# Other priorities for a list-scheduled kernel: attention and two MLPs on one core

## The chip, the cores and the metric

One core of a Trainium2 chip. The metric is the device time of one execution in microseconds (us). The kernel before took 796.75 us, the median of three runs (796.06 to 797.55).

## What is computed

The reference has three parts, one behind the other, all in fp32:

- block-causal attention: 4 batches, 8 heads, 576 positions, 64 channels per head, masked in blocks of 64 positions, softmax over the row;
- an MLP over the 2304 tokens: 512 to 1024 channels, `h * softmax(h)`, a layer norm with the gain `g_ln`, 1024 to 512 channels;
- a second MLP: 512 to 2048 channels, `h * cos(h)`, 2048 to 512 channels.

```python
x = attn(q, k, v)                 # 2304 x 512
h = x @ w_in                      # 2304 x 1024
solu = h * softmax(h)
ln = (solu - mean) / sqrt(var + 1e-6) * g_ln
y = ln @ w_out                    # 2304 x 512
h2 = y @ w2_in                    # 2304 x 2048
out = (h2 * cos(h2)) @ w2_out     # 2304 x 512
```

The weights reach the device as 64-bit words. The kernel turns each piece of 128 x 512 into fp32 and splits it into a high and a low part, and it multiplies activations and weights, both split so, in three products per matmul (high x high, high x low, low x high).

## The kernel before

**A list scheduler writes the order.** Every piece of work is registered with `op(...)` (`Scheduler.op`): the engines that may do it with a planned cost on each, what it reads and writes, and a priority. `Scheduler.run` then plays a planned clock forward. Whenever an engine of the plan is free, `pick` takes from that engine's list the first operation that is ready and whose tiles find a buffer; the list is sorted by the priority less `off(o, e)`, so a lower number goes first. Each engine's instructions are emitted in that order, SP's DMA queue (`q`) included. The order is fixed when the program is built; on the chip an engine never overtakes in its own queue.

The numbers that the plan uses stand in the dictionary `P`:

- `tile`, one number for each of the 18 token tiles of 128, is added to the tile's due time (`tile_pr`). It sets when the first layer (`trace_l1`, line 678), the transposes of the normalised tile (`trace_lnT`, line 711) and, four tiles together, the second layer (`trace_l2`, line 732, with `l2` and `l2_step`) come up.
- `lead0` to `lead7` and `pair` are taken off the due time of one pair of heads in one of eight attention groups; `prep` moves its loads (`trace_prep`) ahead.
- `att_pe`, `att_vec`, `att_slope`, `mlp_pe`, `mlp_vec` shift attention against the first MLP, on TensorE and on the other engines (`off`).
- `w_in`, `w_out`, `w_out_step`, `w2_direct`, `w2_step` are the due times of the weight conversions (`trace_weight`, lines 635 to 649).
- `weight` multiplies the planned costs where an operation may go to one of several engines (`p` TensorE, `s` ACT, `v` VectorE, `g` GpSimd): an engine leaves an operation to another that would end it earlier by these weighted costs. The evictions of the transposes (lines 327 and 331) are such operations.
- `stick` is how far down its list TensorE may look for an operation of the kind that it has just done.

```python
def off(self, o, e):
    kinds = {t.cls for t in o.tiles}
    if kinds & {"rw", "t1", "rwx", "t1x"}:
        return 0.0
    if kinds & {"e1", "LN", "yb", "psh", "st"}:
        return P["mlp_pe"] if e == "p" else P["mlp_vec"]
    if kinds & {"e", "eT", "us", "rq", "rk", "rv", "xs"}:
        return (P["att_pe"] if e == "p" else P["att_vec"]) - P["att_slope"] * o.prio
```

**The stages.** Attention runs in eight groups of four pairs of heads. Groups 0 to 3 are the late 320 rows of the four batches, groups 4 to 7 the early 256 rows (the short groups; their due times start at 200.8, 243.8, 275.8 and 307.8 thousand). A pair loads q, k and v (line 321), scales q (line 333), multiplies q and k (lines 495, 498, 530), takes row maxima (506), exponentials (509), scales them (522 or 524), transposes (581, evicted by 327 or 331) and multiplies with v (606). The result goes into a ring of five tiles XS, `xs_t[n]` in place `n % 5`, from which the first layer reads; tile n of the first layer and tile n + 5 of attention share a place. First-MLP work starts as soon as its tiles are there, and fills TensorE between attention steps. Its results go to DRAM (yD) and come back as chunks of up to 512 tokens.

The second MLP runs in two halves of eight pieces of 128 hidden channels, over five chunks: hidden layer (`trace_h2`, 771), cosine (`trace_cos`: ACT 782, VectorE 783, 785, 787, 789, ACT 791, VectorE 792, then the split at 331 and 336), output (`trace_out`, 811). Its due times start at 373.8 thousand, and each piece of the hidden layer waits for its weights and for the output of four pieces earlier. Its buffers, and most of those of its weights, are opened when the last attention operation has been placed.

The plan knows that VectorE and GpSimd block each other: an operation with `port=True` on VectorE does not start in the plan while a GpSimd one runs, and the reverse.

Where the plan sees TensorE idle before 70 us, small stand-in matmuls (line 953) are emitted.

Of the kernel before, what the change touches and what calls it, by code (L numbers as in the profile page):

```python
# [28 lines left out]


P = {
    "stick": 24783.0,
    "tile": [-14359.3, -37985.7, 6113.4, -3055.7, 24465.2, 4623.7, 3526.9, -32896.1, -22525.7, 27230.1, -18199.6, 22478.0, 37632.5, 59648.4, -15097.6, 596.8, -22562.3, -32058.0],
    "pair": [-10908.6, 3875.9, 1648.0, 792.0],
    "weight": {"p": 1.0, "s": 2.385, "v": 2.75, "g": 1.376, "q": 1.0},
    "att_slope": 0.053,
    "att_pe": 74866.7,
    "att_vec": 151894.2,
    "mlp_pe": -14159.9,
    "mlp_vec": 34158.7,  # L40
    "w_in": -10429.3,
    "w_out": 307495.7,
    "w_out_step": 1138.4,
    "w2_direct": 73027.9,
    "w2_step": 12920.1,
    "lead0": 7512.5,
    "lead1": 22625.7,
    "lead2": 8969.7,
    "lead3": -7974.6,
    "lead4": -9446.8,  # L50
    "lead5": -67400.4,
    "lead6": -7144.6,
    "lead7": -13408.6,
    "l2": 5241.5,
    "l2_step": 15170.5,
    "prep": 36287.5,
}


# [927 lines left out]
```

## Time and profile before

| | |
|---|---|
| time, median of three runs | 796.75 us |
| the profiled execution's own time | 796.97 us |
| its span, first to last instruction | 795.2 us |
| TensorE (PE) busy | 784.4 us, 99% |
| VectorE (DVE) busy | 588.0 us, 74% |
| ACT busy | 421.8 us, 53% |
| GpSimd (POOL) busy | 219.2 us, 28% |
| data moved by DMA | 86.79 MB, mean 109 GB/s |

Busy times are of the profiled execution; matmuls are pipelined, and their ends are modelled. Times within the trace count from the span's start. PEclk is the TensorE clock that was granted, as a share of 2.4 GHz.

### The profile page before, as it was taken

What the parts mean: (1) busy time and instruction counts of PE and PEld (TensorE: products, weight loads), DVE (VectorE), ACT (ScalarE), POOL (GpSimd) and SP (SyncE); (2) the same over time, 40 slices, a digit from 0 to 9 for tenths busy, and PEclk for the clock granted to TensorE, in tenths of its full rate; (3) what the DMA queues carried; (4) which work ended last, traced back from release to release, by engine and by line L of the source; (5) the groups of instructions that cost most, each with busy time, mean ns of one, the idle gap of its engine ahead of it and who ended that gap; (6) DMA issues with size and microseconds to landing.
All of it is one profiled execution on the core that took longest, in us unless ns stands there. A gap on an engine that the chain in (4) does not pass through costs nothing.

```text
span 795.2 us, 12231 instructions
## 1 busy us (share of the span) xinstructions
PE 784.4 (99%) x4291; PEld 622.1 (78%) x4291; DVE 588.0 (74%) x1238; ACT 421.8 (53%) x944; POOL 219.2 (28%) x320
## 2 busy tenths in 40 slices
PE   8999999999999999999999999999999999999998
PEld 5566666767888777889887778889988888888996
DVE  6989998664643774689879999667766676767775
ACT  6987997655433784476354555343434333333332
POOL 2675544412111553555634542000000000000000
PEclk9999999999999999999999999999999999999999
DMA  8435433322112221624385423022415032131121
GB/s 284 155 96 193 138 109 127 109 79 68 41 53 99 81 68 40 234 104 146 115 300 207 133 85 127 11 100 75 149 51 196 3 109 78 54 132 43 51 79 41
DMA packets 46030, 86.79 MB, mean 109 GB/s; under 512 B 4240, under 2 KB 18576, under 8 KB 45968
## 3 DMA queue, kind: packets, MB, share of 16 engines
q1 hardware_dynamic: 45968, 86.00, 32.5%
q8 instruction: 34, 0.56, 0.3%
q14 instruction: 28, 0.23, 0.1%
HBM read 67.11 MB, written 18.87 MB: 108 GB/s over the span
## 4 chain that ended last, share of the span: by engine, by line
PE 86%; DVE 4%; DMA 3%; ACT 2%; POOL 2%; issue 1%; SPq 0%; ACTq 0%; POOLq 0%
PE banks L771 22%; PE banks L811 22%; PE banks L732 13%; PE banks L678 11%; PE banks L606 6%; PE banks L581 5%; PE banks L495 4%; DMA rq<-qT 3%; PE banks L530 2%; PE banks L711 2%; POOL e L524 1%; DVE tr L787 1%; DVE gt L336 1%; DMA rw<-w_out 1%; POOL t L641 0%
## 5 line engine op out<-in xcount | busy, mean ns | idle before, releaser
L678 PE MATMUL banks<-w,XS 128*128 128x512 f32 x432 | 110.5, 401 | 0.0
L331 ACT ACTIVATE gt<-ta 128x512 fp32r<-128x512 f32 (+1 forms) x80 | 47.0, 588 | 110.0 <-PE banks L811 72.0
L732 PE MATMUL banks<-LN,w 128*128 128x512 f32 (+1 forms) x480 | 103.8, 372 | 0.0
L732 PEld LDWEIGHTS banks<-LN,w 128*128 128x128 f32 x480 | 83.1, 189 | 15.1 <-DVE LN L336 0.2
L678 PEld LDWEIGHTS banks<-w,XS 128*128 128x128 f32 x432 | 78.0, 188 | 18.6 <-issue 3.4
L811 PE MATMUL banks<-w,gt 128*128 128x512 f32 x378 | 91.8, 390 | 0.0
L641 POOL TENSOR_TENSOR t<-t,rw 128x512 uint32<-128x512 uint32 x45 | 63.8, 1419 | 80.3 <-DVE t L639 21.4
L782 ACT ACTIVATE ta<-banks 128x512 f32<-128x512 f32 (+1 forms) x80 | 44.3, 554 | 77.5 <-PE banks L771 76.0
L811 PEld LDWEIGHTS banks<-w,gt 128*128 128x128 f32 x378 | 70.8, 188 | 14.1
L783 DVE TENSOR_SCALAR ta<-ta 128x512 f32<-128x512 f32 (+1 forms) x80 | 37.1, 463 | 59.3 <-ACT ta L782 59.1
L509 ACT ACTIVATE e<-banks,us 128x384 f32<-128x384 f32 (+3 forms) x128 | 66.3, 530 | 20.0 <-DVE us L506 18.0
L791 ACT ACTIVATE ta<-tr,hpi 128x512 f32<-128x512 f32 (+1 forms) x80 | 53.9, 673 | 37.5 <-DVE tr L789 37.4
L506 DVE TENSOR_REDUCE us<-banks 128x1 f32<-128x384 f32 (+3 forms) x128 | 56.0, 481 | 14.8 <-PE banks L498 11.0
L336 DVE TENSOR_TENSOR gt<-ta,gt 128x512 fp32r<-128x512 f32 (+1 forms) x80 | 54.0, 675 | 16.4 <-ACT gt L331 15.6
L811 PE MATMUL banks<-wa,gt 128*128 128x512 f32 x270 | 65.7, 390 | 0.0
L792 DVE TENSOR_TENSOR ta<-banks,ta 128x512 f32<-128x512 f32 (+1 forms) x80 | 50.8, 636 | 12.3 <-ACT ta L791 11.9
L581 PE MATMUL banks<-ident,e 128*128 128x128 f32 x400 | 58.7, 278 | 1.1 <-POOL e L524 0.7
L524 POOL TENSOR_SCALAR e<-e,us 128x384 f32<-128x384 f32 (+3 forms) x97 | 49.1, 518 | 37.8 <-ACT e L509 20.4
L331 ACT ACTIVATE eT<-banks 128x512 f32<-128x512 f32 (+3 forms) x104 | 50.4, 525 | 16.0 <-PE banks L581 15.3
L811 PEld LDWEIGHTS banks<-wa,gt 128*128 128x128 f32 x270 | 50.5, 188 | 10.1
L581 PEld LDWEIGHTS banks<-ident,e 128*128 128x128 f32 x400 | 45.4, 140 | 16.0 <-POOL e L524 4.5
L787 DVE SCALAR_TENSOR_TENSOR tr<-ta,tr 128x512 f32<-128x512 f32 (+1 forms) x80 | 55.3, 692 | 2.2
(127 smaller groups left out, 1428.9 us busy)
## 6 DMA issues: line engine op xcount, KB each, us to landing
rw<-w_out SPq DMA_DIRECT2D x24, 512.0 KB, 3.6
rw<-w_in SPq DMA_DIRECT2D x22, 512.0 KB, 3.9
yD<-YB SPq DMA_DIRECT2D x16, 512.0 KB, 2.9
wa<-yD SPq DMA_DIRECT2D x7, 1024.0 KB, 7.6
rk<-kT SPq DMA_DIRECT2D x16, 288.0 KB, 3.7
oD<-ob SPq DMA_DIRECT2D x18, 256.0 KB, 2.4
ob<-oD SPq DMA_DIRECT2D x18, 256.0 KB, 3.3
rv<-vm SPq DMA_DIRECT2D x16, 256.0 KB, 2.9
```

The source lines that it names most:

```text
L331: S.activation(dst, src, AF.Copy, scale=1.0 if scale is None else scale)
L336: (V if eng == "v" else G).tensor_tensor(out=dst, in0=src, in1=h.bitcast(F32), op=ALU.subtract)
L506: op({"v": c_v(W)}, lambda _, h=h: V.tensor_reduce(out=us.ap[:, h:h + 1], in_=scs[h](), axis=AX.X, op=ALU.max, negate=True), [keys[h]], [( ...
L509: op({"s": c_s(W, True, True)}, lambda _, h=h: S.activation(e.ap[:, h, :], scs[h](), AF.Exp, bias=us.ap[:, h:h + 1], scale=1.0, accum_out= ...
L524: G.tensor_scalar(out=a, in0=a, scalar1=us.ap[:, 6 + h:7 + h], scalar2=1.0, op0=ALU.mult, op1=ALU.mult)
L581: PE.transpose(ps.ap[:, 128 * k:128 * k + 128], s(), ident)
L641: op({"g": c_g2(512)}, lambda _: G.tensor_tensor(out=t1.ap, in0=t1.ap, in1=lw(), op=ALU.add), [(rw, 0)], [t1], prio)
L678: PE.matmul(h.ap[:, 512 * c:512 * c + 512], lhsT=xs.ap[:, a, kt, :], rhs=w[:, b, 512 * c:512 * c + 512], start=(kt == 0 and a == 0 and b = ...
L732: PE.matmul(y.ap, lhsT=w[:, a], rhs=LN[:, b, kf, s0_:s0_ + len(t), :], start=(kf == 0 and a == 0 and b == 0), stop=(kf == 7 and b == 1))
L771: PE.matmul(ps.ap, lhsT=w[:, a, 128 * kt:128 * kt + 128], rhs=yts[q, c][kt // 2].ap[:, kt % 2, b, :], start=(k == 0), stop=(k == 11))
L787: op({"v": c_v(n)}, lambda _: V.scalar_tensor_tensor(out=r.ap, in0=a.ap, scalar=-TWO_PI_B, in1=r.ap, op0=ALU.mult, op1=ALU.add), [a], [r], ...
L811: PE.matmul(acc[x][1](), lhsT=gt.ap[:, a, 128 * x:128 * x + 128], rhs=w[:, b, 512:1024], start=(f % 8 == 0 and k == 0), stop=(f % 8 == 7 a ...
```

## The change

Only numbers of `P` differ. No operation, shape, buffer or planned cost is touched; `off`, `pick` and the rest are the same.

```diff
 P = {
-    "stick": 24783.0,
-    "tile": [-14359.3, -37985.7, 6113.4, -3055.7, 24465.2, 4623.7, 3526.9, -32896.1, -22525.7, 27230.1, -18199.6, 22478.0, 37632.5, 59648.4, -15097.6, 596.8, -22562.3, -32058.0],
-    "pair": [-10908.6, 3875.9, 1648.0, 792.0],
-    "weight": {"p": 1.0, "s": 2.385, "v": 2.75, "g": 1.376, "q": 1.0},
-    "att_slope": 0.053,
-    "att_pe": 74866.7,
-    "att_vec": 151894.2,
-    "mlp_pe": -14159.9,
-    "mlp_vec": 34158.7,
-    "w_in": -10429.3,
-    "w_out": 307495.7,
-    "w_out_step": 1138.4,
-    "w2_direct": 73027.9,
-    "w2_step": 12920.1,
-    "lead0": 7512.5,
-    "lead1": 22625.7,
-    "lead2": 8969.7,
-    "lead3": -7974.6,
-    "lead4": -9446.8,
-    "lead5": -67400.4,
-    "lead6": -7144.6,
-    "lead7": -13408.6,
-    "l2": 5241.5,
-    "l2_step": 15170.5,
-    "prep": 36287.5,
+    "stick": 25785.0,
+    "tile": [-37328.3, -83398.7, -19632.4, -6490.1, 22733.9, 11990.0, 16388.8, -15445.7, 4165.2, 47041.7, 14800.1, 26813.9, 32499.4, 56385.3, -32530.7, -2698.7, 16954.9, -23382.4],
+    "pair": [1070.3, 6128.5, 5113.2, 5181.4],
+    "weight": {"p": 1.0, "s": 2.696, "v": 2.758, "g": 1.374, "q": 1.0},
+    "att_slope": 0.1,
+    "att_pe": 78195.4,
+    "att_vec": 59571.4,
+    "mlp_pe": -27189.1,
+    "mlp_vec": -35603.7,
+    "w_in": -7521.5,
+    "w_out": 464087.8,
+    "w_out_step": 22213.3,
+    "w2_direct": 259837.4,
+    "w2_step": 3427.3,
+    "lead0": -2329.2,
+    "lead1": 7670.5,
+    "lead2": -15850.2,
+    "lead3": -6948.8,
+    "lead4": 25932.5,
+    "lead5": -37580.9,
+    "lead6": -18275.3,
+    "lead7": -22786.7,
+    "l2": -13820.7,
+    "l2_step": 12008.3,
+    "prep": 29295.9,
 }
```

## Rows read from the trace of the kernel before

**Rows 1.** The page: busy time of each engine, and the chain by engine.

```profile
PE 784.4 (99%) x4291; PEld 622.1 (78%) x4291; DVE 588.0 (74%) x1238; ACT 421.8 (53%) x944; POOL 219.2 (28%) x320
...
PE 86%; DVE 4%; DMA 3%; ACT 2%; POOL 2%; issue 1%; SPq 0%; ACTq 0%; POOLq 0%
```

**Rows 2.** Stretches: width, busy PE, PEld, DVE, ACT, POOL (instructions), PEclk, DMA share.

```profile
0.00:20.00 20.00, 17.17 (x140) 11.07 (x140) 12.26 (x39) 13.11 (x36) 6.02 (x24) 1.00 0.85 284
20.00:140.00 120.00, 119.45 (x810) 74.86 (x807) 110.98 (x270) 103.67 (x264) 70.11 (x97) 1.00 0.43 135
...
260.00:320.00 60.00, 59.20 (x429) 44.72 (x428) 37.74 (x122) 42.16 (x135) 27.14 (x66) 1.00 0.24 72
...
420.00:480.00 60.00, 57.11 (x248) 46.05 (x247) 56.57 (x88) 32.49 (x56) 27.87 (x22) 1.00 0.44 150
480.00:780.00 300.00, 300.00 (x1403) 258.66 (x1403) 213.23 (x396) 114.01 (x202) 4.93 (x4) 1.00 0.24 80
780.00:795.20 15.20, 11.44 (x53) 9.44 (x52) 8.04 (x15) 3.08 (x6) 0.00 (x0) 0.96 0.14 53
```

**Rows 3.** The chain in order of time: start, us, what; one hidden-layer group.

```profile
602.06 2.72 PE banks L771 x12
```

**Rows 4.** TensorE's waits: engine, line, waited for, us in total, times, longest.

```profile
PE banks L771 <- DVE ta L792: 2.9, 4, 1.4
```

**Rows 5.** Timeline of TensorE, 355 to 405 us: start, us, what.

```profile
381.25 21.92 PE L732 MATMUL banks<-LN,w 128*128 128x512 f32 x96
```

**Rows 6.** Timeline of TensorE, 0 to 20 us; in brackets the idle time before.

```profile
1.97 4.04 PE L953 MATMUL banks<-mrow 128*128 128x128 bf16 x40 [1.97 <-POOL mrow L936]
...
9.13 0.92 PE L495 MATMUL banks<-rk,rq 64*128 64x384 f32 x4 [0.65 <-POOL us L513]
...
10.64 0.40 PE L953 MATMUL banks<-mrow 128*128 128x128 bf16 x4
...
11.21 0.55 PE L953 MATMUL banks<-mrow 128*128 128x128 bf16 x7
```

**Rows 7.** Stretches of line 506 alone, the row maxima: width, busy VectorE (x instructions).

```profile
175.00:217.00 42.00, 4.36 (x14) 1.00 0.21 65
217.00:253.00 36.00, 1.25 (x4) 1.00 0.20 70
253.00:309.00 56.00, 13.06 (x44) 1.00 0.22 65
```

**Rows 8.** Timeline of TensorE, 256 to 300 us, four groups of transposes.

```profile
260.13 1.25 PE L581 MATMUL banks<-ident,e 128*128 128x128 f32 x10
...
267.24 0.82 PE L581 MATMUL banks<-ident,e 128*128 128x128 f32 x6
...
269.28 1.60 PE L581 MATMUL banks<-ident,e 128*128 128x128 f32 x6
...
278.18 2.16 PE L581 MATMUL banks<-ident,e 128*128 128x128 f32 x10
```

**Rows 9.** DMA issues: the short groups' k, KB each, us from issue to landing.

```profile
rk<-kT SPq DMA_DIRECT2D x16, 128.0 KB, 2.3
```

**Rows 10.** Timeline of all engines, 415 to 424 us.

```profile
418.43 1.63 POOL L641 TENSOR_TENSOR t<-t,rw 128x512 uint32<-128x512 uint32 x1 [1.61 <-ACT gt L331]
418.82 1.79 DVE L787 SCALAR_TENSOR_TENSOR tr<-ta,tr 128x512 f32<-128x512 f32 x1
...
423.59 0.70 PE L771 MATMUL banks<-wa,w 128*128 128x512 f32 x2 [1.38 <-DVE ta L792]
```

**Rows 11.** The tile ta: line 787's count, and its duration in ns, min/median/max.

```profile
L787 DVE SCALAR_TENSOR_TENSOR tr<-ta,tr x80: 557/684/1801, 366.6 to 784.8; 128x512 f32<-128x512 f32 x48, 128x384 f32<-128x384 f32 x32
```

**Rows 12.** Timeline of SP's queue, 310 to 332 us: first weight load behind yD's.

```profile
325.68 0.35 SPq L321 DMA_DIRECT2D rw<-w_out  x1
```

**Rows 13.** Lines 331 and 327 in 20 to 140 us: evictions, ns min/median/max.

```profile
L331 ACT ACTIVATE eT<-banks x55: 257/514/626, 21.2 to 139.7; 128x512 f32<-128x512 f32 x27, 128x384 f32<-128x384 f32 x22, 64x128 f32<-64x128 f32 x6
...
L327 DVE COPY eT<-banks x13: 269/558/692, 22.2 to 138.2; 128x512 f32<-128x512 f32 x6, 64x128 f32<-64x128 f32 x5, 128x384 f32<-128x384 f32 x2
```

## The prediction

> **What bounds the kernel now.** I read the head of the page first, with its chain of waits [rows 1]. TensorE is busy for 784.4 of 795.2 us and makes up 86% of the chain that ended last. The reader is to see that this program is one long queue of matmuls, so a new order can win only what TensorE idles, or loses in slow groups. The change adds and removes no matmul of the reference. The profiled execution took 796.97 us, 0.22 above the median of 796.75, and 1.77 of it lies outside the span.
>
> The table of stretches [rows 2] shows where TensorE idles (width less busy): 2.83 us in 0 to 20, 0.55 in 20 to 140, 0.80 in 260 to 320, 2.89 in 420 to 480, nothing in 480 to 780, and 3.76 behind 780, the tail. These six busy times make 664.37 of the 784.4, so the 220 us left out (140 to 260, 320 to 420) are full. From 480 to 780 hidden layer and output alternate at 2.72 us per 12 matmuls [rows 3]: 300 us that no priority reaches. The last sums and stores have nothing to trade places with either. TensorE's own waits [rows 4] put four on VectorE's product at line 792, 2.9 us together.
>
> **The change part by part.** The numbers of P enter the list's rank of each operation (a lower one goes first; I give thousands) and, in `weight`, the choice of engine. From them the plan fixes each engine's order, with that of SP's DMA queue.
>
> Numbers that move nothing: `w_out` goes from 307.5 to 464.1, `w2_direct` from 73.0 to 259.8. The output weights' conversion stands behind the attention then ready with either number. The second MLP's first piece ranks at 373.8+73.0 = 446.8 before and 633.6 after, while the first cosine step ranks at 373.9; whatever is last in a queue stays last. I cost these at nothing. The cover is idle time of VectorE and GpSimd; if a late weight stopped the hidden layer all the same, TensorE has 96 second-layer matmuls, 21.92 us, in one block from 381 us [rows 5], and only a delay beyond that is paid.
>
> Front (0 to 20 us), `lead0`, `lead1`, `pair`, `w_in`: reducible are a wait of 0.65 us and the 11 stand-in matmuls behind the first 40 (0.40 and 0.55), 1.60 us together [rows 6]. The first 1.97 us and the 40 stand-ins cover the first loads and stay. What is left is a dependent chain of load, scaling, scores and exponential, which ranks do not shorten. Bounds: 1.6 gained to 1.0 lost (the wait and half the stand-ins again); I take 0.3, nearer to nothing.
>
> 20 to 140 us: attention's lead over the first MLP on the vector engines falls from 151.9-34.2 = 117.7 to 59.6+35.6 = 95.2, and tiles 0 to 2 come 23 to 45 earlier. `w_in`, first piece at -10.4, stood behind group 2 (-57 to -20) and now, at -7.5, stands ahead of it (54 to 100). First-layer matmuls are thus ready earlier, as filler. At most 0.55 us is left to win; I take 0.2. The loss side is the third rival.
>
> 260 to 320 us: here the order matters most. Of the 64 row maxima of the four short groups (4 to 7), 14 run in 175 to 217 us, 4 in 217 to 253 and 44 in 253 to 309 [rows 7]: a lull, then a crowd. In the crowd ten transposes took 2.16 us where ten took 1.25 just before, and six took 1.60 where six took 0.82 [rows 8]. That is 0.91+0.78 = 1.69 us counted as busy, and with 0.80 idle 2.49 us. After the change group 4's first pair goes from rank 158.0 to 113.0 on TensorE (200.8 less lead and pair, times 1.053 or 1.1, less `att_pe`), group 5's from 264.3 to 230.1. Group 5 stood behind group 6 (234.6); now it precedes it (244.1). Each of these 8 pairs takes its three loads with it, 24 DMAs of about 2.3 us to landing [rows 9]. They pass stores and reloads of y on SP's queue; the DMA engines are 24% busy there [rows 2], so I cost the passing at nothing, and one late load at 2.3 us if that cover fails. The brake is the ring of five xs tiles: group 5 fills tiles 12 and 13, so it waits until tiles 7 and 8 have left, and tile 8's rank goes back from 192.6+14.2 = 206.8 to 219.3+27.2 = 246.5. The lull is filled in part only. Bounds: 2.5 gained to 1.5 lost, for a crowd of the same kind elsewhere; I take 1.3, about half.
>
> 420 to 480 us: VectorE is busy 56.57 of 60 us [rows 2]. TensorE's largest wait there, 1.38 us, follows a VectorE instruction that took 1.79 us, beside a GpSimd step of a weight conversion that had started 0.39 us earlier [rows 10]; the median of that instruction is 0.684, its maximum 1.801 [rows 11]. If attention ends earlier, its buffers are released and the second MLP's conversions, whose first load behind yD's is issued at 325.68 us [rows 12], start earlier and thin out here. Bounds: 2.9 gained to 2.9 lost (the same waits twice); I take 1.0, about a third, because such meetings may only move.
>
> The Trainium skill, "SBUF — State Buffer", section "Who interferes with whom", says that a VectorE instruction with two SBUF inputs and a GpSimd instruction that reads SBUF hold a shared pair of ports for a whole instruction, the one that issues first ahead of the other. By that rule tenths of a microsecond that no plan foresees decide who is blocked; the late term would be 0 and the sum 1.8. The trace agrees with the blocking: the GpSimd step ended at 418.43+1.63 = 420.06, and the stretched instruction 0.55 later, nearly the 0.68 that it takes alone.
>
> Choice of engine: ACT's weight rises from 2.385 to 2.696, VectorE's stays near 2.75. The plan charges 519.5 and 597.5 ns for 512 elements, so VectorE takes a copy when ACT is busy 247 ns longer, against 404 before. I cost this at nothing where VectorE has room, and price it in the third rival where it has none.
>
> Sum: 0.3+0.2+1.3+1.0 = 2.8 us. 796.97-2.8 = 794.17, less 0.22 gives 793.95 on the median: **794.0 us**. All that is recoverable is 1.60+0.55+2.49+2.89 = 7.5 us, or 789.2.
>
> **The rivals.** First, **new meetings eat the gain**. For it: the late wait looked at came from one, and a new order deals them anew. Against it: a lighter stretch has fewer. Two more on TensorE's path at the mean of 2.9/4 = 0.73 us cost 1.5, in place of the 1.0 gained: 796.75-1.8+1.5 = 796.4, the same time. A new list that hardly alters the order ends here too. The Trainium skill's port rule, named above, speaks for this rival.
>
> Second, **the clock falls**. TensorE was granted 1.00, the level of 2.4 GHz, in every stretch but the last, whose mean is 0.96 [rows 2], and a wait of 1.38 us did not lower it. No row shows a wait that did, but one of several us might bring 1.2 GHz; each group of 12 would then take another 2.72 us [rows 3], and two such groups behind a wait of 3 us give 796.75+8.4 = 805. I see no source for such a wait.
>
> Third, **slower: copies move to VectorE between 20 and 140 us**. There VectorE is busy 110.98 of 120 us [rows 2], so 9.02 are free. ACT does 55 evictions of transposed scores there, VectorE 13 at a median of 0.558 us [rows 13]. The point from which it decides is 9.02/0.558 = 16 moved copies. At 22, VectorE is 12.3-9.0 = 3.3 us over; scores wait for their maxima and TensorE with them: 796.75+3.3 = 800. For it: the weight pushes so, and VectorE is the fullest engine beside TensorE. Against: a shift of 157 ns in one choice should move fewer than 16 of 55, and VectorE can take one only when it is free.
>
> **How the numbers follow.** Forecast 0.55; meetings 0.27; copies 0.15; clock 0.03. About 0.2%, or 1.6 us, is what a measurement of this kernel tells from no change: 794.0 lies 2.75 below, 796.4 within, so faster 0.55, same 0.27, slower 0.18. The forecast's own case reaches from 790.5 (most of the 7.5, something left in front and late) to 795.2. For 8 in 10 the range adds the meetings and the lower half of the third rival: 790.5 to 798.6.
>
> **What would show it.** Right: from 260 to 320 under half of the 0.80 idle and no slow transposes; the short groups' maxima spread into 217 to 253; the four waits at line 792 shrunk to about 2 us; the all-matmul stretch from 480 on unchanged in length. The table of stretches, TensorE's waits and the count of maxima answer these one by one. Wrong: new waits of TensorE between 20 and 140 with VectorE above 98%, late waits above 4 us, or a granted clock below 1.00 ahead of the tail.

## The result, and the profile after

The changed kernel took 801.49 us (median of four runs, 801.39 to 801.92) against 796.62 us for the kernel before beside it (796.06 to 797.55). The ratio is 1.0064, with a 95% interval of 1.0052 to 1.0076: slower by 0.64%. The forecast of 794.0 us had the wrong sign, and the time lies above its range. The profiled execution took 801.39 us with a span of 799.4 us, 4.2 us longer than the span before.

The head of the page after, the answer to [rows 1]:

```profile
PE 784.8 (98%) x4291; PEld 622.2 (78%) x4291; DVE 599.6 (75%) x1259; ACT 417.7 (52%) x923; POOL 220.0 (28%) x324
...
PE 77%; DVE 13%; ACT 5%; DMA 2%; issue 2%; POOL 1%; SPq 0%; ACTq 0%; POOLq 0%; DVEq 0%
```

TensorE is as busy as before; the loss is idle time. VectorE's share of the chain that ended last rose from 4% to 13%. The stretches after, with the columns of [rows 2]:

```profile
0.00:20.00 20.00, 17.82 (x138) 11.56 (x140) 11.81 (x38) 13.11 (x36) 5.96 (x24) 1.00 0.85 286
20.00:140.00 120.00, 117.67 (x811) 73.72 (x805) 113.36 (x275) 97.71 (x254) 67.70 (x93) 1.00 0.39 123
...
260.00:320.00 60.00, 59.45 (x404) 44.98 (x401) 44.49 (x138) 41.21 (x129) 29.95 (x68) 1.00 0.32 99
320.00:420.00 100.00, 97.80 (x500) 82.92 (x500) 75.37 (x129) 56.21 (x90) 40.58 (x39) 1.00 0.35 120
420.00:480.00 60.00, 57.50 (x253) 46.94 (x251) 55.92 (x84) 30.20 (x51) 25.73 (x23) 1.00 0.60 216
480.00:780.00 300.00, 298.98 (x1391) 256.45 (x1392) 218.45 (x400) 114.32 (x202) 10.59 (x9) 1.00 0.24 81
780.00:799.40 19.40, 15.69 (x75) 13.29 (x73) 10.98 (x22) 4.61 (x9) 0.00 (x0) 0.98 0.11 41
```

TensorE's idle time (width less busy) grew from 0.55 to 2.33 us in 20 to 140, from nothing to 2.20 in 320 to 420, from nothing to 1.02 behind 480, and from nothing to 0.15 in 140 to 260. It shrank from 2.83 to 2.18 in front, from 0.80 to 0.55 in 260 to 320 and from 2.89 to 2.50 in 420 to 480; the tail is the same (3.71 against 3.76). So there are three places to explain. TensorE's waits after, the answer to [rows 4]:

```profile
PE banks L771 <- DVE ta L792: 4.6, 5, 1.8
...
PE banks L711 <- DVE ta L792: 1.1, 1, 1.1
PE banks L581 <- DVE e L522: 0.8, 2, 0.5
PE banks L581 <- ACT e L539: 0.8, 2, 0.6
```

Waits on VectorE's product at line 792 doubled, from 2.9 to 5.7 us. The timeline of all engines shows one instance of each new loss:

```profile
60.30 2.04 DVE L522 TENSOR_SCALAR e<-e,us 128x512 f32<-128x512 f32 x2
60.59 1.46 POOL L641 TENSOR_TENSOR t<-t,rw 128x512 uint32<-128x512 uint32 x1
...
63.31 1.49 PE L581 MATMUL banks<-ident,e 128*128 128x128 f32 x11 [0.60 <-ACT e L539]
...
371.97 0.42 DVE L789 TENSOR_SCALAR tr<-tr 128x512 f32<-128x512 f32 x1
372.31 1.28 ACT L791 ACT_TABLE_LOAD   x1
373.60 0.72 ACT L791 ACTIVATE ta<-tr,hpi 128x512 f32<-128x512 f32 x1
374.36 0.69 DVE L792 TENSOR_TENSOR ta<-banks,ta 128x512 f32<-128x512 f32 x1 [1.04 <-ACT ta L791]
375.20 1.06 PE L711 MATMUL banks<-ident,E 128*128 128x128 f32 x8 [1.08 <-DVE ta L792]
...
450.03 1.63 POOL L641 TENSOR_TENSOR t<-t,rw 128x512 uint32<-128x512 uint32 x1 [3.88 <-ACT ob L331]
450.41 1.80 DVE L336 TENSOR_TENSOR gt<-ta,gt 128x512 fp32r<-128x512 f32 x1
...
452.13 0.83 DVE L789 TENSOR_SCALAR tr<-tr 128x512 f32<-128x512 f32 x1
453.00 0.72 ACT L791 ACTIVATE ta<-tr,hpi 128x512 f32<-128x512 f32 x1 [1.74 <-DVE tr L789]
453.76 0.69 DVE L792 TENSOR_TENSOR ta<-banks,ta 128x512 f32<-128x512 f32 x1 [0.20 <-ACT ta L791]
454.50 1.88 PE L771 MATMUL banks<-w,w 128*128 128x512 f32 x7 [1.79 <-DVE ta L792]
```

At 60 and at 450 us it is the meeting of [rows 10] again: a GpSimd step starts beside a VectorE one, the VectorE instruction ends only behind it (1.80 us instead of its usual 0.68), and what follows on VectorE, ACT and TensorE waits with it. At 372 us it is something that the prediction does not have: ACT loads a table ahead of a sine, and the product and the transposes wait for it. ACT's table loads, by line, with count, busy us, mean ns and idle time ahead, first in the kernel before:

```profile
L509 ACT ACT_TABLE_LOAD x1 | 1.3, 1283 | 0.7 <-PEq L980 0.7
L791 ACT ACT_TABLE_LOAD x1 | 1.3, 1283 | 0.0
```

The same groups in the kernel after:

```profile
L791 ACT ACT_TABLE_LOAD x3 | 3.8, 1283 | 0.1
L683 ACT ACT_TABLE_LOAD x2 | 2.6, 1283 | 0.0
L509 ACT ACT_TABLE_LOAD x1 | 1.3, 1283 | 0.7 <-PEq L980 0.7
```

Before, ACT goes once from exponentials to sines. After, the exponentials of the first MLP's last tiles (line 683) alternate with the first sines (791): five loads, at 352.2, 356.6, 361.9, 365.3 and 372.3 us. The numbers say why. On ACT, tile 16's exponential ranked at 339.8-22.6-34.2 = 283.0 thousand; it now ranks at 339.8+17.0+35.6 = 392.4. Tile 13's goes from 291.8+59.6-34.2 = 317.2 to 291.8+56.4+35.6 = 383.8. The first cosine step stays at 373.9, so both exponentials now stand behind a sine, and each brings a switch and a switch back. The plan charges no table load, so on its clock the interleaving costs nothing.

**How far the chip runs behind the plan.** The scheduler's own clock gives a planned start for every operation, so each TensorE operation has a drift: its start on the chip, counted from the span's start, less its planned start. The difference of two kernels' times is the difference of their plans and of their final drifts. In us, drift at the first operation behind each time:

```
               plan    140    360    385    500    end
before        787.35   3.11   4.49   4.43   8.00   9.06
after         788.36   4.10   4.50   7.08  11.63  12.30
```

The plan itself became 1.0 us longer, and the drift 3.2 longer: +1.0 up to 140, -1.0 from 140 to 360, +2.6 from 360 to 385 (where the table loads are), +1.0 from 385 to 500, -0.4 behind. That is the whole 4.2 us of span. A drift is that of the one profiled execution of its kernel.

### The profile page after: what moved, and what is told of

It reads as the page before. It is cut to its first block, busy times and chain, and to the rows that moved or that the text cites. A ratio compares the mean times of both kernels' runs of the same rounds, so it can differ in the third digit from the quotient of the medians.

```text
span 799.4 us, 12272 instructions
## 1 busy us (share of the span) xinstructions
PE 784.8 (98%) x4291; PEld 622.2 (78%) x4291; DVE 599.6 (75%) x1259; ACT 417.7 (52%) x923; POOL 220.0 (28%) x324
## 4 chain that ended last, share of the span: by engine, by line
PE 77%; DVE 13%; ACT 5%; DMA 2%; issue 2%; POOL 1%; SPq 0%; ACTq 0%; POOLq 0%; DVEq 0%
PE banks L811 20%; PE banks L771 19%; PE banks L732 12%; PE banks L678 10%; PE banks L581 5%; PE banks L606 5%; PE banks L495 3%; PE banks L530 2%; PE banks L711 2%; DVE tr L787 1%; DVE gt L336 1%; DVE us L506 1%; DVE t L639 1%; DMA rq<-qT 1%; DVE tr L785 1%
## 5 line engine op out<-in xcount | busy, mean ns | idle before, releaser
L811 PE MATMUL banks<-w,gt 128*128 128x512 f32 x432 | 104.6, 390 | 0.0
L732 PE MATMUL banks<-LN,w 128*128 128x512 f32 (+1 forms) x480 | 100.7, 369 | 0.0
L811 PEld LDWEIGHTS banks<-w,gt 128*128 128x128 f32 x432 | 80.8, 188 | 16.2
L783 DVE TENSOR_SCALAR ta<-ta 128x512 f32<-128x512 f32 (+1 forms) x80 | 34.7, 433 | 59.2 <-ACT ta L782 58.7
L509 ACT ACTIVATE e<-banks,us 128x256 f32<-128x256 f32 (+3 forms) x128 | 66.4, 529 | 21.0 <-DVE us L506 18.1
L524 POOL TENSOR_SCALAR e<-e,us 128x128 f32<-128x128 f32 (+3 forms) x104 | 59.4, 584 | 61.4 <-DVE us L515 46.9
L506 DVE TENSOR_REDUCE us<-banks 128x1 f32<-128x512 f32 (+3 forms) x128 | 56.2, 482 | 16.8 <-PE banks L498 13.4
L771 PE MATMUL banks<-wa,w 128*128 128x512 f32 (+1 forms) x288 | 64.5, 372 | 1.1 <-DVE ta L792 1.1
L771 PEld LDWEIGHTS banks<-wa,w 128*128 128x128 f32 x288 | 53.0, 188 | 9.6 <-DVE ta L792 1.6
L787 DVE SCALAR_TENSOR_TENSOR tr<-ta,tr 128x512 f32<-128x512 f32 (+1 forms) x80 | 53.6, 670 | 2.2
```

What stands on the lines that cost most here:

```text
L506: op({"v": c_v(W)}, lambda _, h=h: V.tensor_reduce(out=us.ap[:, h:h + 1], in_=scs[h](), axis=AX.X, op=ALU.max, negate=True), [keys[h]], [( ...
L509: op({"s": c_s(W, True, True)}, lambda _, h=h: S.activation(e.ap[:, h, :], scs[h](), AF.Exp, bias=us.ap[:, h:h + 1], scale=1.0, accum_out= ...
L524: G.tensor_scalar(out=a, in0=a, scalar1=us.ap[:, 6 + h:7 + h], scalar2=1.0, op0=ALU.mult, op1=ALU.mult)
L732: PE.matmul(y.ap, lhsT=w[:, a], rhs=LN[:, b, kf, s0_:s0_ + len(t), :], start=(kf == 0 and a == 0 and b == 0), stop=(kf == 7 and b == 1))
L771: PE.matmul(ps.ap, lhsT=w[:, a, 128 * kt:128 * kt + 128], rhs=yts[q, c][kt // 2].ap[:, kt % 2, b, :], start=(k == 0), stop=(k == 11))
L787: op({"v": c_v(n)}, lambda _: V.scalar_tensor_tensor(out=r.ap, in0=a.ap, scalar=-TWO_PI_B, in1=r.ap, op0=ALU.mult, op1=ALU.add), [a], [r], ...
```

## The experiments

Beside the three sets of runs below, the kernel before took 797.01, 796.54 and 796.84 us. A gain is a difference of medians (for the changed kernel, from 801.49); the ratio is to the kernel before of the same set, and its 95% interval reaches 0.6 us or more to either side.

**One table, both kernels.** At line 791 the sine becomes an exponential, so that every ACT function comes from one table; list and plan are unchanged.

```diff
-        op({"s": c_s(n, True)}, lambda _: S.activation(cs.ap, r.ap, AF.Sin, bias=hpi, scale=1.0), [r], [cs], prio)
+        op({"s": c_s(n, True)}, lambda _: S.activation(cs.ap, r.ap, AF.Exp, bias=hpi, scale=1.0), [r], [cs], prio)
```

> The changed kernel with its sine replaced by an exponential at line 791: same instructions, same order, same engines, but ACT stays in one function table, so the four extra table loads of 1.28 us between 356 and 374 us (and the first one at 352) are gone. What it computes in the cosine is not cos. Theory A (table loads between the last tiles' exponentials and the first sines cost TensorE's waits of 1.1 and 1.1 us behind line 792 at 375 and 380 us): 2.0 to 2.6 us faster than the changed kernel's 801.5, so 799.0 to 799.5, with those two waits gone or under 0.3 us together. Theory B (VectorE is overloaded there by copies taken from ACT): ACT's loads are beside the path, and the time stays at 801.0 to 801.9.

> The kernel before with the same replacement of sine by exponential. It has a single table load, at 366.0 us, ahead of the first sine, while TensorE has the second layer of the first MLP to do. Theory A: within 0.5 us of the kernel before, 796.2 to 796.9. If sine were simply slower to evaluate than the exponential (a rival reading of the run beside it), this one would gain too: about as much as the other.

After with it: 798.50 us, 3.0 less, ratio to the kernel before 1.0019 (1.0010 to 1.0028). Before with it: 796.94 us beside 797.01, ratio 0.9999 (0.9990 to 1.0008). The stretch from 360 on, in the changed kernel with one table:

```profile
360.00:420.00 60.00, 60.00 (x320) 51.82 (x319) 45.20 (x79) 27.47 (x47) 23.25 (x21) 1.00 0.38 124
```

TensorE is full from 360 to 420 (57.80 with the tables), and the wait of line 711 is gone; the waits on line 792 that stay are four of 3.4 us together. So the added table loads cost 3.0 us, a little more than was expected and some 60% of the loss; the one load that the kernel before needs costs nothing that a run shows. What follows too: with the tables out of the way the changed kernel is still not faster than the one before.

**GpSimd kept behind VectorE.** The plan lets a GpSimd operation start only when no VectorE operation that uses the shared port is running, but nothing in the emitted program holds it there: each engine starts when its own inputs are ready. This edit gives a GpSimd operation one more wait, for the last port-using VectorE instruction planned ahead of it (of several GpSimd operations in a row, only the first needs it). The helpers return their instruction for it; that part of the edit is left out here.

```diff
+    def behind(o, ins, held):
+        if o.eng == "g" and held is not None:
+            tc.add_manual_dep(ins.ins, held.ins.name,
+                              mybir.DependencyInfo(mybir.DependencyClass.Sync, mybir.DependencyReason.SCHED_ONLY), reason="port")
+        return ins if o.eng == "v" and o.port else None if o.eng == "g" else held
...
-            o.fn(o.eng)
+            held = behind(o, o.fn(o.eng), held)
```

> The changed kernel, each GpSimd instruction made to wait for the last port-using VectorE instruction that the plan puts ahead of it: same instructions in the same order on every engine, only waits added on GpSimd. Theory A2 (GpSimd steps, ready earlier than planned, take the shared port ahead of their turn and stretch VectorE on TensorE's path): stretched VectorE instructions (over 1.0 us where 0.68 is usual) fall to a third or fewer, TensorE's idle time between 20 and 140 us falls from 2.33 to about 1.2 and between 420 and 500 from 3.5 to under 1.5 us, and the time to 798.0 to 799.5. Rival B (VectorE has simply too much to do, 113.4 of 120 us early and 58 of 60 late): the stretch disappears but the waits stay; 801 to 802. Rival C (the added waits make the weights late): slower, 802 to 806.

> The kernel before with the same added waits on GpSimd. Theory A2: the four waits behind line 792 between 420 and 480 us (2.9 us) shrink to under 1.0 and the time falls by 1.5 to 3 us, to 793.5 to 795.2. Rival B: no change, 796 to 797. Rival C: slower by 1 us or more.

After with it: 798.19 us, 3.3 less, ratio 1.0017 (1.0008 to 1.0026). Before with it: **794.33 us**, 2.7 less, ratio 0.9967 (0.9954 to 0.9979). That is the fastest version of the study: faster than the kernel before by 0.33% and than the changed one by 7.2 us. In the kernel before with it, the timeline at the place of [rows 10], where the same GpSimd step had started at 418.43, 0.39 us ahead of line 787:

```profile
418.33 0.80 DVE L639 SCALAR_TENSOR_TENSOR t<-t,rw 128x512 uint32<-128x512 uint32 x1
...
419.66 0.68 DVE L787 SCALAR_TENSOR_TENSOR tr<-ta,tr 128x512 f32<-128x512 f32 x1
...
421.41 1.32 POOL L641 TENSOR_TENSOR t<-t,rw 128x512 uint32<-128x512 uint32 x1 [2.82 <-ACT ta L782]
```

And its stretch from 420 on:

```profile
420.00:500.00 80.00, 80.00 (x353) 65.74 (x352) 74.35 (x123) 45.22 (x75) 27.77 (x26) 1.00 0.40 132
```

The GpSimd step now starts behind line 787, line 787 takes 0.68 us again, TensorE is busy all 80 us (77.11 before), and no wait on line 792 is left. In the changed kernel the wait on line 792 falls to 2.4 us (the tables are still there), and the one on GpSimd's scaling (line 524) grows from 0.4 to 2.1 us, the price of holding it back.

The meetings themselves do not go away. Of the instructions at lines 336, 787 and 639 that take over 1.0 us, 17 become 13 before and 24 become 12 after; a fall to a third had been expected. Line 787 in the kernel before with the port waits, against [rows 11]:

```profile
L787 DVE SCALAR_TENSOR_TENSOR tr<-ta,tr x80: 557/682/1794, 366.8 to 782.2; 128x512 f32<-128x512 f32 x48, 128x384 f32<-128x384 f32 x32
```

Between 420 and 500 us eight of these instructions still take over 1.0 us, where eleven did, and TensorE waits for none of them. A meeting in the planned order stays; what the waits take out is the one in which GpSimd comes ahead of its turn. No run adds as many waits in another order, so that the order does it, and not a slower GpSimd, is read from the traces.

**Both edits at once**, in the changed kernel:

> The changed kernel with both repairs: sine replaced by an exponential (no second function table; the cosine is not computed) and GpSimd waiting for the VectorE instruction planned ahead of it. Theory A (two causes in different places, 356 to 381 us and 20 to 140 with 440 to 500 us): the two gains add, 801.5-3.0-3.3 = 795.2, so 794.6 to 795.9, and about 1 us is left to the repaired kernel before (794.3), which is what the plan itself lost. Rival D (one cause seen twice: either repair only gives the late stretch slack): the gains overlap, 797 to 798.

It took 796.40 us, ratio 0.9999 (0.9990 to 1.0008): 5.1 less, where the two add to 6.3, and half a us above what was expected. Whether the gains overlap is not settled: with these intervals the medians allow both, and by the final drifts below the gains are 3.2 and 2.5 singly and 5.7 together. It stays 2.1 us behind the kernel before with the waits alone, of which 1.0 is the longer plan. Drift of all these, in us:

```
                            plan    140    360    385    500    end
before, port waits         787.35   3.03   5.37   5.48   5.36   6.43
after, one table           788.36   3.98   4.08   3.97   8.47   9.14
after, port waits          788.36   3.27   5.00   7.41   9.11   9.77
after, both                788.36   3.35   4.34   4.21   5.89   6.57
after, tile 16             788.36   4.22   4.60   6.85  13.46  14.18
after, tile 16, port waits 788.36   2.82   4.69   6.45   8.69   9.35
before, after's weights    792.18   9.80  11.04  10.80  16.94  18.22
```

One table takes out the rise from 360 to 385. The port waits take 0.8 out ahead of 140, and most of the rise from 385 to 500. With both, the changed list drifts no more than the better old one (6.57 against 6.43 at the end), in an execution that took 0.8 us less than its median.

**Fewer table loads by a number.** Tile 16's entry goes from 16954.9 to 8000.0. The plan is as long as before the edit, and ACT switches three times in place of five: tile 16's exponential now ranks at 383.4, beside tile 13's 383.8, and both are still behind the first sine.

```diff
-    "tile": [..., -32530.7, -2698.7, 16954.9, -23382.4],
+    "tile": [..., -32530.7, -2698.7, 8000.0, -23382.4],
```

> The changed kernel with one number altered: tile 16's goes from 16954.9 to 8000.0, between the old value (-22562.3) and the new. The plan is as long to the nanosecond and differs only between 343 and 383 us of its clock; ACT changes its table 3 times there instead of 5. Theory A: two of the four extra loads go, and with them 1.0 to 2.0 us: 799.5 to 800.5. Rival (the order of the last tiles costs for another reason, say VectorE's load there): 801.0 to 802.0.

> The same altered number together with GpSimd's added waits. Theory A: both gains, 801.5-1.4-3.3 = 796.8, so 796.2 to 797.5: no better than the kernel before (797.0 in the runs beside the last ones), and 2 to 3 us behind the kernel before with the same waits. Rival D: 798 or more.

Both missed: 803.26 us, ratio 1.0085 (1.0071 to 1.0099), and with the port waits 798.39 us, ratio 1.0025 (1.0014 to 1.0036). ACT's timeline in the first:

```profile
352.31 1.28 ACT L791 ACT_TABLE_LOAD   x1
...
356.71 1.28 ACT L683 ACT_TABLE_LOAD   x1
...
370.29 1.28 ACT L791 ACT_TABLE_LOAD   x1
```

Drift from 360 to 385 fell only from 2.6 to 2.2: the load at 370.3 stands where the one at 372.3 stood, on the path, and the two that went had been beside other work. Here it is where a load falls that sets its price, and not how many there are. The rise from 385 to 500 grew from 4.6 to 6.6, and the port waits take it back to 2.2: new meetings. So a change of one number, with a plan of the same length, moved 1.8 us the wrong way by the meetings; with the port waits the difference is gone (798.39 against 798.19).

**The engine weights alone, in the kernel before.**

```diff
-    "weight": {"p": 1.0, "s": 2.385, "v": 2.75, "g": 1.376, "q": 1.0},
+    "weight": {"p": 1.0, "s": 2.696, "v": 2.758, "g": 1.374, "q": 1.0},
```

> The kernel before with the new choice-of-engine weights alone (ACT 2.696 for 2.385). This is the prediction's third rival by itself: copies go from ACT to VectorE. By that rival 799 to 801, with VectorE over 113 of 120 us busy between 20 and 140 and TensorE idle there 3 us or more. The plan itself is 4.8 us longer with it, of which 3.7 idle between 20 and 100 us of its clock, since the other numbers were not fitted to it: 800.5 to 803. If the weights do nothing alone: 796 to 797.5.

It took 809.33 us, ratio 1.0158 (1.0140 to 1.0176), more than either theory gave. Its plan is 4.8 us longer, so one group of numbers in the other list is no step towards the change. VectorE was not overloaded in 20 to 140, the third rival's mechanism: it was busy for 103.33 us there, less than before. Instead TensorE idled for 6.57 us there, of which 3.74 stand in the plan, and the clock fell:

```profile
60.00:61.00 1.00, 0.59 (x4) 0.09 (x3) 1.00 (x3) 1.00 (x4) 0.91 (x2) 1.00 0.00 0
61.00:62.00 1.00, 0.00 (x0) 0.00 (x0) 1.00 (x2) 0.25 (x1) 0.38 (x2) 1.00 0.57 131
62.00:63.00 1.00, 0.65 (x4) 0.42 (x4) 1.00 (x2) 0.04 (x1) 1.00 (x1) 0.87 0.94 381
63.00:64.00 1.00, 0.30 (x2) 0.33 (x3) 1.00 (x4) 0.56 (x1) 0.91 (x2) 0.50 0.04 12
64.00:66.00 2.00, 2.00 (x10) 1.08 (x10) 0.63 (x3) 0.60 (x1) 0.03 (x1) 0.50 0.00 0
```

(The columns are those of [rows 2].) The granted clock stays at 0.50, the 1.2 GHz level, until between 69 and 70 us. On TensorE's timeline the 40 matmuls of line 606 take 7.05 us there, against 4.78 for 40 of the kernel before at 103.96.

**Later weights.** The runs with late weights in the changed kernel and in the old one ask whether the full VectorE is to blame. Both kernels convert the second half's weights (pieces 8 to 15) while the first half runs, which is where the late meetings are. Here each such conversion is registered behind a hidden-layer step, so that 9 or 10 of their 16 GpSimd steps run behind 500 us.

```diff
-    for f in range(16):
+    def trace_w2(f, after):
...
+    for f in range(8):
+        trace_w2(f, ())
...
+            if k in range(12, 28, 2):
+                trace_w2(8 + (k - 12) // 2, [("h2", k)])
```

> The changed kernel with the second half's weight conversions spread out: piece 8 is released behind hidden-layer step 12, piece 9 behind step 14, and so on, so that they run from about 445 to 535 us and not from 400 to 505. They are needed from 587 us on. The plan is 0.06 us longer. Theory A3 (the late waits need VectorE nearly full, and the crowd of conversions that nobody needs yet makes it so): TensorE's idle time between 420 and 500 falls from 3.5 to under 1.5 us without any added wait, and the time by 2 to 3.5 us, to 798.0 to 799.5. Rival E (each meeting of GpSimd and VectorE costs the same wherever it falls): the idle time moves to 500 to 540 and the time stays at 801 to 802.

> The kernel before with the same spreading; its plan is 0.2 us longer. Theory A3: the 2.9 us of waits between 420 and 480 fall to under 1.2, and the time to 794.3 to 795.6. Rival E: 796.3 to 797.3.

> The changed kernel with the spreading and with GpSimd's added waits. Theory A3: most of the late loss is the same one that the added waits remove, so the two gains overlap: 797.0 to 798.4, against 798.2 with the waits alone; what is left to the kernel before's repaired time is the table loads (about 2.5 us) and the plan (1.0 us). Rival E: 798.2 or more.

> The kernel before with the spreading and GpSimd's added waits: the version meant to beat both kernels. The late waits are already 0 with the added waits alone (794.3), so the spreading can add nothing there: 794.0 to 794.8, 2 us or more under the kernel before.

After, late: 801.09 us, ratio 1.0047 (1.0035 to 1.0059); before, late: 796.18, 0.9987 (0.9979 to 0.9996). With the port waits as well: after 798.22, 1.0015 (1.0007 to 1.0023); before 796.81, 0.9996 (0.9986 to 1.0006). The kernel before with late weights, 420 to 500 and 500 to 600:

```profile
420.00:500.00 80.00, 78.37 (x345) 64.24 (x344) 65.23 (x108) 39.62 (x66) 16.63 (x14) 1.00 0.30 106
500.00:600.00 100.00, 99.33 (x480) 87.10 (x478) 85.94 (x158) 49.13 (x89) 22.02 (x20) 1.00 0.33 113
```

VectorE went from 75.05 to 65.23 busy of 80 us, half of GpSimd's work there left, and TensorE's idle time only fell from 2.89 to 1.63, with 0.67 new behind 500. In the changed kernel, where most of the late loss had been expected to go, 420 to 500 improves by 1.9 us and 500 to 600 loses 1.67. That is rival E for the changed kernel; the kernel before gained 0.7 us, between the two theories, and 798.22 fits both. TensorE's waits fell about as GpSimd's work did and came back in part where that work went, with 15 us of VectorE's time free: a full VectorE is not the cause. The last run missed its expectation: with late weights the port waits gained nothing (796.81 against 796.18). Its trace shows two new waits on line 792 in 500 to 600, 1.2 us together, and its plan is 0.2 longer. That covers the 1.2 us by which its profiled execution (795.56) stands above that of the port waits alone; its median stands 2.5 above, and why is open.

## Why the prediction was wrong

**The step that failed is the one that leaves 320 to 420 us out of the sum as full.** TensorE does not idle there before, so the prediction priced no loss in it, and it made no term of ACT's switches between functions. After the change TensorE idles for 2.20 us there, and not at all from 360 to 420 with one table. The comparison that was needed stands in the prediction: "Numbers that move nothing" ranks the late weights' conversions against the first cosine step at 373.9. About the numbers that it names it is right: with the old values of `w_out`, `w_out_step`, `w2_direct` and `w2_step` the changed kernel's scheduler writes the same order, operation by operation. But the same comparison for the entries of `tile`, which stand in the diff, and for `mlp_vec`, whose sign turns, puts the exponentials of tiles 13 and 16 at 383.8 and 392.4, behind that step. One exponential behind one sine means a switch of ACT's function and back. The table loads stood in the trace of before, 1.28 us of ACT each, and were put at nothing without a word. They cost 3.0 us, shown by the run with one table. The Trainium skill, "ScalarE: Activation LUTs", section "What ACT_TABLE_LOAD costs", gives 1283 ns for a load and about 1380 ns for a drain with each switch; the trace agrees on the load, and shows no drain as an item of its own.

The busy times that the prediction adds up make 564.37 us, not 664.37; its conclusion, that the 220 us left out are full, follows from the right sum.

**420 to 480 us, +1.0: wrong.** The cause named was right: the waits come from meetings of VectorE and GpSimd, and the waits that keep GpSimd in its planned place remove them all in the kernel before. But the stretch did not thin out. The second MLP's conversions go on 9 us earlier, as was said (line 641 at 315.1 us in place of 324.3), and yet end 11 us later (last at 499.5 in place of 488.2). The steps of line 641 in 420 to 500 (width, busy GpSimd and its instructions, then as in [rows 2]), first in the kernel before:

```profile
420.00:500.00 80.00, 17.59 (x12) 1.00 0.39 132
```

The same stretch in the kernel after:

```profile
420.00:500.00 80.00, 19.22 (x14) 1.00 0.51 182
```

TensorE's idle time is 2.50 against 2.89 us in 420 to 480, and 1.02 more behind 480. The step said itself that "such meetings may only move", and took a third of them as gain all the same; the drift from 385 to 500 came out 1.0 worse.

**20 to 140 us, +0.2: wrong.** Idle time rose by 1.78. Part is the plan: its own TensorE idle time in the stretch grew by 0.56 us, from 0.05. Most of the rest is meetings, as at 60.3 us: with port waits in both kernels the drift at 140 differs by 0.24 us, without them by 0.99. The third rival's road to a loss, copies to VectorE, was not taken: 18 evictions of scores on VectorE against 13 [rows 13], 7 of the XS copies against 2, VectorE busy 113.36 of 120 us, and 19.52 of 20 us in the fullest sixth.

**260 to 320 us, +1.3: little of it came.** Idle time fell from 0.80 to 0.55, not under half, and slow transposes remain (six take 1.28 us at 272.19, where six took 0.82 before). The drift from 140 to 360 came out 1.0 us better, but only 0.4 of it behind 260; what made the rest, where TensorE had no idle time before, is open. The maxima of line 506 thinned out, though less than was said, the answer to [rows 7]:

```profile
175.00:217.00 42.00, 5.94 (x14) 1.00 0.24 74
217.00:253.00 36.00, 2.39 (x8) 1.00 0.17 59
253.00:309.00 56.00, 12.21 (x40) 1.00 0.22 65
```

The lull holds 8 in place of 4, the crowd 40 in place of 44.

**Front, +0.3: not kept.** The wait of 0.65 us is gone, but the 40 stand-ins took 4.45 us in place of 4.04, and the lead is used up by 40 us, where both kernels drift by 2.7.

**480 us to the end:** unchanged as said, but for 1.02 us of waits in 480 to 500, where weights are still being converted.

**The rivals.** The first, new meetings, happened: they took the late gain, and with the tables away TensorE's waits at line 792 are 3.4 us against 2.9. Its price of two more waits, 1.5 us, is not what was measured: the port waits are worth 3.3 us in the changed kernel and 2.7 in the old, and the 0.6 between them lies within the intervals. The prediction priced meetings as a gain lost, not as a cost that the kernel before already paid. The Trainium skill, "SBUF — State Buffer", section "Who interferes with whom", says that issue order decides who is blocked; the runs with enforced order agree (line 787 at the place of [rows 10] takes 0.68 us in place of 1.79). The clock did not fall in the changed kernel (1.00 ahead of the tail).

So two causes of the loss are known: table loads, 3.0 us, measured by an edit with its control, and a plan 1.0 us longer. The other 0.9 of the 4.87 us stays open. Meetings are worth 0.6 us more in the new list, but that is not clear of noise, and the better drift from 140 to 360 stands against it.

## What to carry to other kernels

A planner optimises what it prices: when only its priorities change, rank each moved operation against the neighbours on its engine, and ask which cost between them (here a table load) the planner leaves out. An order that the plan assumes between two engines has to be enforced on the chip by a wait; one more dependency on GpSimd's instructions was worth 2.7 us in the kernel before and 2.9 to 4.9 in the changed one and its two variants, more than any re-ranking here, though nothing in the kernel before with late weights. Planned start against measured start, operation by operation, shows where a plan and a chip part, and the plan's own length shows what is lost before the chip comes into it.

## What the runs showed of the hardware

- A table load on ACT takes 1283 ns each time, and its cost in the kernel's time runs from nothing (the one ahead of the sines in the kernel before) to about the 1.1 us that TensorE waited behind the one at 372.3 us.
- TensorE's granted clock fell to 0.50, the 1.2 GHz level, at about 63 us behind a wait of 1.68 us, with short pieces of work around it (run with the weights alone), and not behind a wait of 1.79 us at 452.7 us between full groups in the changed kernel. The prediction had asked for a wait of several us.
- A VectorE instruction of 0.68 us takes up to 1.80 us beside a GpSimd step. With late weights in the kernel before, TensorE's idle time in 420 to 500 us fell about as GpSimd's busy time did (2.89 to 1.63 us for 32.79 to 16.63) and not as VectorE's (75.05 to 65.23). With the order enforced in it, line 787 still reached 1794 ns, and TensorE had no wait there: a meeting cost time where GpSimd came ahead of its planned turn.
